# Sliding-window attention with a highway layer: keys on the partitions, values over 128 rows, a cast v that is moved on chip

## The chip, the cores and the metric

The kernel runs on one core of one Trainium2 chip. The metric is the device time of one execution in microseconds; the kernel before took 182.04 us (median of 3 runs, 181.88 to 184.85). TensorE (PE in the profile) multiplies, VectorE (DVE), ScalarE (ACT) and GpSimd (POOL) work on elements, SyncE (SP) only issues DMAs here. Each engine takes its instructions strictly in the order in which they were written for it.

## The reference

```python
B, H, S, D = 8, 8, 576, 64                 # q, k, v: float32
scores = q @ k.T / sqrt(D)
rel = pos[:, None] - pos[None, :]          # query minus key
slopes = 2.0 ** (-8.0 * (arange(H) + 1) / H)
mask = (rel >= 0) & (rel < 128)            # causal, a window of 128
attn = softmax(where(mask, scores - slopes * abs(rel), -1e9))
x = (attn @ v) as (4608, 512)              # heads side by side
H = relu(x @ w_h)                          # w_h, w_t: 512 x 512
T = sigmoid(x @ w_t + b_t)
out = T * H + (1 - T) * x                  # float32
```

A query sees its own key and the 127 before it, so a tile of 128 keys matters to 256 queries at most.

## The kernel before, in words

The work is cut into batches b (8) and, in a batch, key tiles u of 128 keys (u = 0 to 3, and u = 4 with 64 keys: 40 units) and output blocks of 128 tokens. There are 36 blocks: four whole ones a batch, and a fifth (tau = 4) for each pair of batches, which holds the last 64 tokens of both. All matrices are bf16.

Loads. `load_qk` (L115 to L123) fetches q and k on POOL's DMA queue and turns them to bf16 on the way; `load_v` (L125) fetches v as float32 on SP's queue, two neighbouring tokens in each partition; `cast_v` (L132) turns it to bf16 in the tile `va`, which has a column of ones beside each head so that the row sums of the softmax come out of the same matmul. `tr` (L216) transposes q and k on DVE, so that 32 pairs of features stand on the partitions of each head: four heads j fill 128 partitions, h says which four.

Scores, `scores` (L227). For a unit, 32 matmuls of 32 rows by 64 columns of the array (L235): t picks the even or the odd keys, e the half of the features, h the half of the heads. The 64 keys of one t stand on 64 partitions of PSUM, and h decides which 64. Then 16 matmuls of 32 by 32 (L244) add the mask and the ALiBi slope from a table. The result takes four PSUM banks (`sc`, one buffer), so the scores of a unit can't begin before the exponential of the last unit has read them. `soft` (L250) is that exponential on ACT, PSUM to bf16.

Values, `pv` (L265). A block takes the unit of its own tokens and the one before. Since the even and odd keys of four heads stand on 64 partitions, its matmuls (L287) are 64 rows deep: 32 for a block with two units, 16 for tau = 0, 64 for tau = 4. `norm` (L299) divides by the row sums on DVE, `x_tr` (L308) transposes the block by four matmuls, `x_copy` (L314) takes that to SBUF on ACT or DVE. The tile `av` (PSUM, one buffer) holds both the values and the transposed block.

The highway layer. `mm_z` (L333) and `mm_h` (L344) are four matmuls of 128x512 each. The bias enters z by a copy on ACT before them (`bias`, L319) or by a matmul (`bias_mm`, L323). Then `tanh` on ACT, `relu_sub`, `to_gate`, `gate` and `add_x` on DVE and POOL, and `store` (L367) on SP's queue.

What sets the order. The string ORDER (L14) is a list of words written out by hand, one for each step above: the letter names the step (S scores, E exponential, P values, N norm, U transpose, X or x copy on ACT or DVE, Z or z the z matmuls with the bias by ACT or by matmul, H, Y tanh, R, O, G or g, A or a, D store, T transposes of q and k, C or c cast of v, V, Q, L loads), the digits its place. Nothing reorders it. On SP's queue the loads of v and the stores stand in one line, and a store that waits for its block holds back all that is behind it.

Of the kernel before, what the change touches and what calls it, by code (L numbers as in the profile page):

```python
# [9 lines left out]
P = 128  # L10
NB, NU, NJ = 8, 5, 4
# [3 lines left out]
Q011 V000 V001 V011 V010 J L02 L10 L12 i0 Q010 i1 Q000 Q001 L00 K I T0111 T0100 T0101 T0110 V021  # L15
T0001 T0000 T0011 V020 T0010 V030 M S00 V031 F C01 E00 c00 w02 S01 w03 W11 w10 Q111 P00 E01 N00
Q100 U00 X00 S02 W00 P01 E02 W01 N01 W13 H00 V200 Q101 T1111 U01 S03 Q110 X01 R00 W12 E03 T1110
H01 V120 V110 V100 V101 T1001 C02 V111 P02 T1000 z00 N02 T1011 S04 Y00 U02 R01 z01 X02 V121
T1010 H02 C03 V130 T1101 Y01 V040 Q21 E04 T1100 P03 V131 Q20 O01 S10 V221 N03 V141 E10 C10 V041
g01 U03 z02 x03 A01 O00 R02 V140 Y02 G00 P10 S11 N10 B03 A00 H03 E11 O02 g02 U10 A02 T2101 Z03  # L20
T2110 X10 S12 C11 R03 V201 Y03 C12 P11 E12 O03 z10 N11 G03 T2100 U11 A03 H10 X11 V211 T2000 D00
Y10 P12 V210 R10 B11 S13 D02 N12 V220 V400 H11 C14 V300 E13 O10 D01 C13 T2111 U12 Z11 V311 G10
T2011 X12 D03 S14 Y11 R11 V310 P13 Q31 E14 T2001 z12 V301 A10 N13 V240 H12 V230 Y12 Q30 T2010
U13 C04 O12 S20 X13 O11 R12 G11 P14 E20 z13 N14 A11 c20 U14 Y13 G12 S21 x14 T3111 P20 E21 A12
z14 N20 C22 D12 H13 V231 T3100 D10 C21 Y14 O13 U20 R13 S22 X20 T3110 B20 G13 P21 E22 D11 Z20 N21
A13 H14 O14 T3011 Q40 D13 V340 V320 U21 V321 S23 R14 X21 V401 Y20 T3010 P22 G14 V420 E23 z21 N22
A14 T3001 U22 S24 X22 C23 T3000 H20 Y21 C31 T3101 E24 P23 C30 O20 B22 S30 R20 Q41 N23 H21 G20
E30 O21 U23 Z22 R21 A20 g21 X23 S31 T4001 A21 Y22 P30 T4000 E31 z23 D21 V330 V421 N30 V331 V410
H22 T4011 Y23 U30 O22 C32 V411 S32 X30 R22 V440 P31 T4010 G22 E32 V241 z30 N31 V341 A22 D14 O23
U31 H23 T4110 D20 X31 C33 V431 c42 Y30 P32 Q50 R23 B31 S33 N32 G23 H30 E33 O30 U32 A23 R30 Z31  # L30
X32 T4100 S34 C24 D23 D22 V521 V430 P33 T4101 E34 G30 H31 N33 Y31 A30 z32 R31 T4111 H32 C34 Y32
O31 Q51 U33 g31 S40 X33 R32 A31 O32 P34 E40 g32 D31 V501 V540 V601 T5000 V500 z33 A32 V610 D30
N34 H33 C43 D32 Y33 C40 O33 U34 S41 R33 X34 C41 B34 T5001 G33 P40 H34 E41 N40 A33 V511 Z34 T5011
V510 V541 U40 R34 Q61 S42 V731 X40 T5010 D33 C50 Y34 P41 V710 E42 O34 z40 T5100 G34 N41 H40 A34
Y40 T5111 U41 S43 X41 R40 Q60 z41 E43 O40 T5101 G40 P42 T5110 S44 A40 N42 H41 E44 Y41 T6101 D40
U42 V520 V730 S50 X42 R41 P43 O41 E50 G41 z42 N43 V611 c51 A41 U43 D34 Y42 S51 x43 V630 O42 P50
V441 E51 z43 N50 V640 T6110 V531 U50 H42 C52 V600 Y43 T6010 V530 X50 S52 R42 V621 P51 T6100 G42
E52 V631 z50 N51 V620 D41 A42 T6111 U51 H43 X51 O43 Q70 Y50 P52 R43 C61 B51 S53 N52 G43 Z51 E53
T6011 C53 U52 H50 T6001 A43 X52 O50 S54 Y51 R50 P53 Q71 E54 z52 N53 C44 C54 V741 V641 V700 D42
g50 V701 H51 Y52 T6000 A50 U53 O51 S60 X53 R51 C73 B53 P54 g51 E60 O52 A51 H52 N54 Z53 C60 D51  # L40
V711 R52 V740 D43 V721 U54 T7000 G52 S61 X54 T7010 Y53 P60 A52 T7001 H53 E61 N60 C62 z54 D52 D50
C63 O53 R53 U60 S62 X60 g53 Y54 T7110 A53 P61 E62 z60 N61 C70 T7101 U61 C74 H54 Y60 O54 X61 S63
R54 P62 T7011 E63 G54 z61 N62 A54 T7111 S64 H60 E64 T7100 D54 D53 V720 Y61 U62 O60 S70 R60 X62
B62 g60 P63 O61 A60 E70 H61 N63 Z62 C64 R61 U63 g61 Y62 H62 a61 X63 O62 S71 B63 R62 P70 E71 g62
H63 N70 A62 Z63 R63 C71 D62 D61 D60 U70 Y63 S72 C72 x70 O63 P71 E72 g63 z70 N71 A63 U71 H70 D63
X71 Y70 P72 R70 B71 S73 N72 H71 E73 O70 g70 U72 Z71 A70 x72 R71 P73 Y71 D70 S74 N73 z72 E74 O71
g71 U73 Y72 H72 x73 A71 O72 P74 R72 D71 z73 N74 G72 U74 Y73 A72 H73 x74 z74 R73 D72 O73 H74 g73
Y74 A73 O74 R74 D73 g74 a74 D74
# [4 lines left out]
def kernel(  # L53
# [27 lines left out]
    NEG = 1.0e6  # L81
# [19 lines left out]
    VA = [cp.tile([P, NU, NJ, 2, D + 1], BF16, name=f"va{i}") for i in range(4)]  # L101

    PR = [cp.tile([P, NJ, 2, 256], BF16, name=f"pr{i}") for i in range(5)]
    PS = [cp.tile([P, NJ, 2, 256], BF16, name=f"ps{i}") for i in range(2)]
# [5 lines left out]
    ident = cp.tile([P, P], BF16, name="ident")  # L110

    SI = cp.tile([P, 2, 32], BF16, name="si")
    MT = cp.tile([P, 2, 320], BF16, name="mt")
# [18 lines left out]
    def cast_v(b, u, eng):  # L132
        eng.tensor_copy(  # L133
            out=VA[b % 4][:, u, :, :, 0:D],
            in_=VS[b % 3][:, u].rearrange("p j (t d) -> p j t d", t=2))
# [16 lines left out]
    def split_b():  # L152

        nc.vector.memset(one[:], 1.0)
        nc.vector.memset(bR[:], 0.0)
# [278 lines left out]
```

## Time and profile before

| | |
|---|---|
| time, median of 3 runs | 182.04 us |
| the profiled execution's own time | 180.61 us |
| its span, first to last instruction | 178.7 us |
| mean granted clock of TensorE | 0.981 |
| busy: PE, DVE, ACT, POOL | 141.2, 131.7, 103.7, 100.8 us |
| matmuls that the trace holds | 3490 |
| moved by DMA | 31.17 MB, 224 GB/s of HBM traffic |

The time of a run is about 1.9 us more than the span of its profile, which covers the instructions alone. Busy time is summed over the whole span, so it mixes the start (loads), a long steady part and the end (the last blocks). Matmuls are pipelined: a busy PE may still be waiting for weights, and a row's duration is longer than the distance from one row's start to the next. That distance is what the engine spends.

### The profile page before, as it was taken

Reading aid. Unit: us, or ns where it says so; the run is one execution under the profiler, and the core shown is the slowest. Engines: PE = TensorE matmul, PEld = TensorE weight load, DVE = VectorE, ACT = ScalarE, POOL = GpSimd, SP = SyncE. Lnnn points to the kernel's source line nnn. Section 1 sums busy time; section 2 is a strip of 40 time slices with the busy share of each in tenths; the row PEclk is TensorE's granted clock in tenths of the full one; section 3 lists DMA queues with packets and bytes.
Section 4 is the critical chain, followed back from the end, with each engine's and each line's share of the span. In section 5 each row is a group of like instructions: output and inputs, shape, how many; then the busy total and the mean of one; then the engine's idle time right before and its main releaser. Section 6 shows DMA issues by size and latency. Waiting matters only on the chain.

```text
span 178.7 us, 7880 instructions
## 1 busy us (share of the span) xinstructions
PE 141.2 (79%) x3490; PEld 80.8 (45%) x3529; DVE 131.7 (74%) x276; ACT 103.7 (58%) x117; POOL 100.8 (56%) x125
## 2 busy tenths in 40 slices
PE   0004559988999897699998998999779999999940
PEld 0002335544556454355555555545455555555510
DVE  4757938977886877277989986578669778857680
ACT  2000557566877687188755885778375858775210
POOL 6203590067797679536858986349576653522720
PEclk9999999999999999699999999999999999999996
DMA  4999999993789759905998999948986305151132
GB/s 79 215 259 369 217 171 223 227 188 106 226 188 183 201 168 205 189 31 178 166 299 147 286 187 257 280 138 207 162 212 199 121 4 150 55 187 62 59 117 61
DMA packets 30641, 31.17 MB, mean 174 GB/s; under 512 B 2320, under 2 KB 20752, under 8 KB 30608
## 3 DMA queue, kind: packets, MB, share of 16 engines
q1 hardware_dynamic: 26192, 21.24, 40.1%
q0 software_dynamic: 4416, 9.44, 32.1%
q8 instruction: 27, 0.44, 1.0%
q14 instruction: 6, 0.05, 0.1%
HBM read 30.67 MB, written 9.44 MB: 224 GB/s over the span
## 4 chain that ended last, share of the span: by engine, by line
PE 75%; issue 8%; DMA 6%; DVE 5%; POOL 2%; ACT 1%; POOLq 0%
PE h L348 18%; PE z L336 17%; PE av L287 13%; PE sc L235 12%; PE sc L244 7%; DMA ld<-in_q_dram 6%; PE av L311 5%; PE z L325 3%; ACT pr L258 1%; POOL ld L121 1%; DVE wH L147 1%; DVE vs L205 1%; DVE va L133 0%; DVE wT L147 0%; DVE tr L218 0%
## 5 line engine op out<-in xcount | busy, mean ns | idle before, releaser
L258 ACT ACTIVATE pr<-sc 128x2048 bf16<-128x2048 f32 (+2 forms) x32 | 53.3, 1664 | 37.6 <-PE sc L244 37.6
L365 POOL TENSOR_TENSOR ot<-uu,x 128x512 f32<-128x512 bf16 x34 | 39.4, 1158 | 26.6 <-DVE uu L361 16.4
L218 DVE STREAM_TRANSPOSE tr<-ld 128x288 uint32<-128x288 uint32 x64 | 41.9, 707 | 4.0 <-DMA ld<-in_k_dram 2.6
L235 PE MATMUL sc<-tr,tr 32*64 32x256 bf16 (+2 forms) x1280 | 27.5, 280 | 19.1 <-DVE tr L218 15.9
L348 PE MATMUL h<-wH,xt 128*128 128x512 bf16 x128 | 36.9, 386 | 1.2 <-issue 0.6
L336 PE MATMUL z<-wT,xt 128*128 128x512 bf16 x128 | 34.0, 379 | 2.1 <-issue 1.2
L361 POOL TENSOR_TENSOR uu<-uu,tt 128x512 bf16<-128x512 bf16 x20 | 23.1, 1156 | 17.0 <-DVE uu L353 12.3
L133 POOL CAST va<-vs 128x512 bf16<-128x512 f32 x36 | 21.8, 627 | 17.6 <-DMA vs<-in_v_dram 17.6
L353 DVE SCALAR_TENSOR_TENSOR uu<-h,x 128x512 bf16<-128x512 f32 x36 | 24.7, 687 | 9.0 <-PE h L348 8.4
L342 ACT ACTIVATE tt<-z 128x512 f16<-128x512 f32 x36 | 21.5, 598 | 15.2 <-PE z L336 15.0
L235 PEld LDWEIGHTS <-tr 32*64 32x64 bf16 x1280 | 17.8, 140 | 27.1 <-issue 12.7
L287 PE MATMUL av<-va,pr 64*128 64x65 bf16 (+1 forms) x960 | 23.1, 195 | 5.9 <-issue 5.4
L304 DVE TENSOR_TENSOR x<-av,rd 128x512 bf16<-128x512 f32 x36 | 24.9, 692 | 1.3
L287 PEld LDWEIGHTS <-pr 64*128 64x128 bf16 (+1 forms) x960 | 18.3, 98 | 14.2 <-issue 9.0
L316 ACT COPY xt<-av 128x512 bf16<-128x512 bf16 x29 | 17.0, 585 | 10.8 <-PE av L311 9.9
L303 DVE RECIPROCAL rd<-av 128x8 f32<-128x8 f32 x36 | 7.3, 202 | 20.7 <-PE av L287 20.5
L336 PEld LDWEIGHTS <-xt 128*128 128x128 bf16 x144 | 13.7, 98 | 13.6 <-issue 0.9
L357 DVE TENSOR_SCALAR tt<-tt 128x512 f16<-128x512 f16 x36 | 17.8, 497 | 2.3 <-ACT tt L342 2.2
L348 PEld LDWEIGHTS <-xt 128*128 128x128 bf16 x144 | 12.6, 99 | 13.5 <-issue 2.3
L244 PE MATMUL sc<-mt,si 32*32 32x512 bf16 (+2 forms) x640 | 16.5, 364 | 0.0
L311 PE MATMUL av<-ident,x 128*128 128x128 bf16 x144 | 14.3, 222 | 2.4 <-DVE x L304 1.9
L311 PEld LDWEIGHTS <-x 128*128 128x128 bf16 x144 | 10.1, 99 | 11.9 <-DVE x L304 5.7
(46 smaller groups left out, 82.6 us busy)
## 6 DMA issues: line engine op xcount, KB each, us to landing
vs<-in_v_dram SPq DMA_DIRECT2D x64, 128.0 KB, 5.1
out_dram<-ot SPq DMA_DIRECT2D x32, 256.0 KB, 3.3
ld<-in_k_dram POOLq DMA_DIRECT2D x6, 576.0 KB, 7.5
ld<-in_q_dram POOLq DMA_DIRECT2D x6, 576.0 KB, 8.1
ld<-in_k_dram POOLq DMA_DIRECT2D x4, 288.0 KB, 6.2
ld<-in_q_dram POOLq DMA_DIRECT2D x4, 288.0 KB, 8.0
vs<-in_moe_w_h_dram SPq DMA_DIRECT2D x2, 512.0 KB, 12.6
vs<-in_moe_w_t_dram SPq DMA_DIRECT2D x2, 512.0 KB, 12.1
```

Source lines behind the costliest of these rows:

```text
L218: nc.vector.transpose(out=t[:, 0:S, :].rearrange("p s e -> p (s e)").bitcast(U32).rearrange("p (s t) -> p t s", t=NT)[:, 9 * part : 9 * pa ...
L235: nc.tensor.matmul(out=sc[64 * h : 64 * h + 64, j, 256 * t : 256 * t + n], lhsT=TR[b % 2, 1, h][rows, k0 : k0 + 127 : 2, e], rhs=TR[b % 2, ...
L244: nc.tensor.matmul(out=sc[32 * c : 32 * c + 32, j, :].rearrange("p (t n) -> p t n", t=2)[:, :, 0:n], lhsT=SI[rows, c // 2, :], rhs=MT[rows ...
L258: nc.scalar.activation(out=p[:, :, :, 0:n], in_=SC.pop((b, u))[:].rearrange("p j (t n) -> p j t n", t=2)[:, :, :, 0:n], func=ACTF.Exp, sca ...
L287: nc.tensor.matmul(out=av[o : o + m, h, 65 * j : 65 * j + 65], lhsT=PT[bb, u][rows, j, 1 - t, off : off + m], rhs=VA[bb % 4][rows, u, j, t ...
L304: nc.vector.tensor_tensor(out=x[:].rearrange("p (h j d) -> p h j d", h=2, j=NJ), in0=av[:, :, :, 0:D], in1=rd[:].to_broadcast([P, 2, NJ, D ...
L311: nc.tensor.transpose(out=AV[blk][:, c // 2, 272 + 64 * (c % 2) :][:, 0:64].bitcast(BF16), in_=X[blk][:, c * P : (c + 1) * P], identity=id ...
L336: nc.tensor.matmul(out=pz[:], lhsT=xt[:, c * P : (c + 1) * P], rhs=wT[:, c, :], start=False, stop=c == NC - 1, skip_group_check=True)
L348: nc.tensor.matmul(out=pa[:], lhsT=xt[:, c * P : (c + 1) * P], rhs=wH[:, c, :], start=c == 0, stop=c == NC - 1)
L353: nc.vector.scalar_tensor_tensor(out=uu[:], in0=PA.pop(blk)[:], scalar=0.0, in1=X[blk][:], op0=ALU.max, op1=ALU.subtract)
L361: eng.tensor_tensor(out=UU[blk][:], in0=UU[blk][:], in1=TT.pop(blk)[:], op=ALU.mult)
L365: eng.tensor_tensor(out=ot[:], in0=UU.pop(blk)[:], in1=X.pop(blk)[:], op=ALU.add)
```

## The change

It does five things.

**Keys on the partitions.** A unit's 128 keys now stand on the 128 partitions of PSUM in their own order. A score matmul is 32 rows by 128 columns of the array (L248), so there are 16 of N = 256 for a unit where there were 32. The mask and bias table is built for this order (`mt`), and its slope is in the table instead of in the weights.

**Units 3 and 4 in one.** The last 64 keys of a batch share the PSUM tile of unit 3: 16 matmuls of N = 192, 16 of N = 64, one set of 16 bias matmuls (from a table of its own, `mx`), one exponential. There are 32 units instead of 40, all with 2048 columns.

**Values over 128 rows.** `pv` (L306) uses all 128 partitions: 16 matmuls for a block with two units, 8 for tau = 0, 32 for tau = 4, the last ones 64 columns wide, in two column halves that alternate.

**A cast v that is moved.** v still comes with two neighbouring tokens in each partition, but keys now stand one in each partition. So `cast_v` writes a tile `vg`, and `move_v` (44 DMAs on SP's queue) carries it to `va`, 64 rows a DMA: token parity t goes to every second partition. 12 of the 40 casts are on ACT, 28 on POOL (before: 4 on DVE, 36 on POOL).

**Another order of issue.** Most q and k transposes are one instruction instead of two (28 whole, 8 halves; before 64 halves). 14 x copies are on DVE instead of 7, 20 bias copies on ACT instead of 11 (so 16 bias matmuls instead of 25). There are four buffers `pr` and one `ps`, before five and two. The clearing of buffers moves from DVE to POOL.

On PE, what stands about the last units of batch 0, before (h is the highway matmul, av the values or the transposes, si the bias weights, mt the bias table; rows that alternate are left out):

```order
L311 MATMUL av<-ident,x 128x128
L235 LDWEIGHTS tr_87
L235 MATMUL sc<-tr_85,tr_87 64x192
...
L244 MATMUL sc<-mt,si 32x2x192
L348 LDWEIGHTS xt
...
L235 MATMUL sc<-tr_85,tr_87 64x64
...
L244 MATMUL sc<-mt,si 32x2x64
L311 LDWEIGHTS x
```

and of the change:

```order
L306 MATMUL av<-va_98,pr_102 128x65
L248 LDWEIGHTS tr_87
L248 MATMUL sc<-tr_85,tr_87 128x192
...
L248 MATMUL sc<-tr_86,tr_88 128x64
L258 LDWEIGHTS eye
L258 MATMUL sc<-mx,eye 32x512
L324 LDWEIGHTS x
```

Two visits to the scores, each with its own bias matmuls, have become one.

On SP's queue, from the first store of a pair's shared block on (batches 0 and 1), before (vs is v as loaded, ot a finished block):

```order
L376 DMA out_0_dram<-ot_1659 64x512 x2
L372 DMA out_0_dram<-ot_1840 128x512
L127 DMA vs1_94<-in_v_dram 64x4x128
L372 DMA out_0_dram<-ot_2176 128x512
L372 DMA out_0_dram<-ot_2050 128x512
```

and of the change, there and a little later:

```order
L389 DMA out_0_dram<-ot_1400 64x512 x2
L385 DMA out_0_dram<-ot_1342 128x512
L143 DMA va0_98<-vg0_96 64x1300 x2
L132 DMA vs2_95<-in_v_dram 64x4x128
L385 DMA out_0_dram<-ot_1435 128x512
L132 DMA vs2_95<-in_v_dram 64x4x128
L143 DMA va0_98<-vg0_96 64x1300
```

The four moves of a batch stand in the same line as the stores and the loads. From batch 2 on each carries the whole batch's 5 units for one parity and one half of the heads.

On POOL, the start, before:

```order
L121 DMA ld01_80<-in_k_dram 128x1152
L174 ISA
L174 IOTA pi_115 32x1 x4
L176 IOTA qi_116 128x321
L177 AFFINE_SELECT ident_112<-ident_112 128x128
L121 DMA ld01_80<-in_k_dram 128x1152
L121 DMA ld00_79<-in_q_dram 128x1152 x2
```

and of the change:

```order
L217 MEMSET vs_94 128x512
L217 MEMSET vs_93 128x512
L126 DMA ld_79<-in_q_dram 128x1152 x2
L226 MEMSET vg_96 128x40
L226 MEMSET vg_97 128x40
L180 ISA
L180 IOTA pi 32x1 x4
L182 IOTA qi 128x352
L183 AFFINE_SELECT ident<-ident 128x128
L126 DMA ld_80<-in_k_dram 128x1152 x2
```

Two clears now stand ahead of the first load of q, and the loads of k behind the index tables.

The diff, cut to its core (the ORDER string is replaced as a whole; its first line is shown):

```diff
-Q011 V000 V001 V011 V010 J L02 L10 L12 i0 Q010 i1 Q000 Q001 L00 K I T0111 T0100 T0101 T0110 V021
+i2 L02 M1 V001 M0 V000 Q001 J V011 Q000 V041 I V040 i0 V031 V021 Q011 i1 L10 Q010 W02 F c00 f
...
-    VA = [cp.tile([P, NU, NJ, 2, D + 1], BF16, name=f"va{i}") for i in range(4)]
+    VG = [cp.tile([P, 2, NU, NJ, D + 1], BF16, name=f"vg{i}") for i in range(2)]
+    VA = [cp.tile([P, 2, NU, NJ, D + 1], BF16, name=f"va{i}") for i in range(4)]
...
     def cast_v(b, u, eng):
-        eng.tensor_copy(
-            out=VA[b % 4][:, u, :, :, 0:D],
-            in_=VS[b % 3][:, u].rearrange("p j (t d) -> p j t d", t=2))
+        (eng.copy if eng is nc.scalar else eng.tensor_copy)(
+            out=VG[b % 2][:, :, u, :, 0:D],
+            in_=VS[b % 3][:, u].rearrange("p j (t d) -> p t j d", t=2))
+
+    def move_v(b, u0, u1, t, half):
+        nc.sync.dma_start(
+            out=VA[b % 4][t::2, half, u0:u1].rearrange("r u j d -> r (u j d)"),
+            in_=VG[b % 2][64 * half : 64 * half + 64, t, u0:u1].rearrange("r u j d -> r (u j d)"))
...
     def scores(b, u):
         sc = SC[b, u] = ps_sc.tile([P, NJ, 512], F32, name="sc")
-        n = min(256, S - P * u)
-        for t in range(2):
+        parts = [(u, 0, 256)] if u < 3 else [(3, 0, 192), (4, 192, 64)]
+        for kt, col, n in parts:
             for e in range(2):
                 for h in range(2):
                     for j in range(NJ):
...
-                            out=sc[64 * h : 64 * h + 64, j, 256 * t : 256 * t + n],
-                            lhsT=TR[b % 2, 1, h][rows, k0 : k0 + 127 : 2, e],
-                            rhs=TR[b % 2, 0, h][rows, P * u : P * u + n, e],
...
-                            tile_position=(32 * j, 64 * h))
+                            out=sc[:, j, 256 * h + col : 256 * h + col + n],
+                            lhsT=TR[b % 2, 1, h][rows, P * kt : P * kt + P, e],
+                            rhs=TR[b % 2, 0, h][rows, P * kt : P * kt + n, e],
...
+                            skip_group_check=True, tile_position=(32 * j, 0))
...
-                    lhsT=SI[rows, c // 2, :], rhs=MT[rows, :, off : off + n], start=False,
...
+                    lhsT=eye[rows, :],
+                    rhs=MT[rows, :, off : off + 256] if u < 3 else MX[rows, c],
...
     def pv(blk):
...
-                lhsT=PT[bb, u][rows, j, 1 - t, off : off + m],
-                rhs=VA[bb % 4][rows, u, j, t, :], start=first, stop=True,
-                skip_group_check=True, tile_position=(64 * h, o))
...
+                out=av[o : o + m, h, 65 * j : 65 * j + 65], lhsT=PT[bb, pt][:, j, h, off : off + m],
+                rhs=VA[bb % 4][:, h, u, j, :], start=(h, o) not in seen, stop=True,
+                skip_group_check=True, **kw)
```

More of the change, by code (lines that the diff above doesn't have):

```diff
@@ L10 @@
 P = 128
[L11 removed]
+NB, NU, NJ, NPR = 8, 5, 4, 4
 ORDER = """
[L15 to L19 removed]
@@ L207, in k_clear, with v_clear @@
+    def v_clear(b):
+        nc.gpsimd.memset(VS[b][:, 4], 0.0)
     def k_clear():
@@ L263, with warm @@
+    def warm(n):
+        pz = ps_f.tile([P, DM], F32, name="z")
+        for _ in range(n):
+            nc.tensor.matmul(out=pz[:], lhsT=one[:], rhs=nil[:], start=True, stop=True)
     PZ, XT, PA, TT, UU, OT = {}, {}, {}, {}, {}, {}
     def pv(blk):
-        calls = []
-        b, tau = blk
-        if True:
-            av = AV[blk] = ps_av.tile([P, 2, 512], F32, name="av")
-            terms = [(b, tau, 0, 0, P)]
-            if tau:
-                terms.append((b, tau - 1, P, 0, P))
-            if tau == 4:
-                terms = [(bb, u, off, 64 * i, 64) for i, bb in enumerate((b - 1, b))
-                         for u, off in ((4, 0), (3, P))]
-            seen = set()
-            for bb, u, off, o, m in terms:
-                for j in range(NJ):
-                    for t in range(2):
-                        for h in range(2):
-                            calls.append((bb, u, off, o, m, j, t, h, (h, o) not in seen))
-                            seen.add((h, o))
@@ L285, in one_mm @@
[L285 to L297 removed]
+        b, tau = blk
```

225 lines of the change are left out of this document (120 added, 105 removed).

## The prediction

> **What bounds the kernel now.** First the page: its parts on busy time and on the chain that ended last.
>
> ```profile
> span 178.7 us, 7880 instructions
> PE 141.2 (79%) x3490; PEld 80.8 (45%) x3529; DVE 131.7 (74%) x276; ACT 103.7 (58%) x117; POOL 100.8 (56%) x125
> PE 75%; issue 8%; DMA 6%; DVE 5%; POOL 2%; ACT 1%; POOLq 0%
> ```
>
> DVE's share is almost PE's, but the chain is PE for 75% and "issue" for 8% more, so the shares don't say who waits. The view of waits on PE does:
>
> ```profile
> PE sc L235 <- DVE tr L218: 15.9, 2, 14.0
> PE av L287 <- issue: 5.4, 4, 2.4
> PE sc L235 <- ACT pr L258: 2.0, 1, 2.0
> PE av L311 <- DVE x L304: 1.9, 1, 1.9
> PE z L336 <- issue: 1.2, 7, 0.2
> PE sc L235 <- issue: 1.2, 2, 0.6
> PE h L348 <- issue: 0.6, 3, 0.2
> PE av L287 <- ACT pr L258: 0.5, 1, 0.5
> ```
>
> The timeline puts the first, third and fourth of these into the start, and shows where the start and PE's work end:
>
> ```profile
> 14.04 0.43 PE L235 MATMUL sc<-tr,tr 32*64 32x256 bf16 x4 [14.04 <-DVE tr L218]
> 16.31 1.07 PE L235 MATMUL sc<-tr,tr 32*64 32x256 bf16 x28 [1.84 <-DVE tr L218]
> ...
> 20.00 1.08 PE L235 MATMUL sc<-tr,tr 32*64 32x256 bf16 x32 [2.04 <-ACT pr L258]
> ...
> 24.12 0.61 PE L311 MATMUL av<-ident,x 128*128 128x128 bf16 x4 [1.90 <-DVE x L304]
> ...
> 170.85 1.03 PE L348 MATMUL h<-wH,xt 128*128 128x512 bf16 x4
> ```
>
> Between 24.1 and 171.9 us PE waits for another engine once, 0.5 us. What is left is its own work and "issue". So a microsecond less on PE there is a microsecond less in the end, as long as the others keep up. What that work costs is read from starts, not from durations:
>
> ```profile
> 81.05 0.39 PE L311 MATMUL av<-ident,x 128*128 128x128 bf16 x4
> 81.37 0.69 PE L235 MATMUL sc<-tr,tr 32*64 32x256 bf16 x32
> 81.99 0.43 PE L244 MATMUL sc<-mt,si 32*32 32x512 bf16 x16
> 82.35 0.69 PE L287 MATMUL av<-va,pr 64*128 64x65 bf16 x32
> ...
> 84.08 0.40 PE L311 MATMUL av<-ident,x 128*128 128x128 bf16 x4
> 84.31 1.03 PE L348 MATMUL h<-wH,xt 128*128 128x512 bf16 x4
> 85.27 0.69 PE L287 MATMUL av<-va,pr 64*128 64x65 bf16 x32
> 85.89 0.58 PE L235 MATMUL sc<-tr,tr 32*64 32x192 bf16 x32
> 86.40 0.38 PE L244 MATMUL sc<-mt,si 32*32 32x384 bf16 x16
> 86.72 1.04 PE L348 MATMUL h<-wH,xt 128*128 128x512 bf16 x3
> 87.59 0.39 PE L311 MATMUL av<-ident,x 128*128 128x128 bf16 x4
> ...
> 88.77 0.45 PE L235 MATMUL sc<-tr,tr 32*64 32x64 bf16 x32
> 89.15 0.27 PE L244 MATMUL sc<-mt,si 32*32 32x128 bf16 x16
> 89.35 0.69 PE L287 MATMUL av<-va,pr 64*128 64x65 bf16 x32
> ```
>
> From start to start: scores of a whole unit 0.62, its bias matmuls 0.36; unit 3 0.51 and 0.32; unit 4 0.38 and 0.20; values 0.62; four highway matmuls 0.87 (one of the four is missing at 86.72), 0.22 each. The four transposes cost 0.23 before dense matmuls (84.08) but 0.32 before scores (81.05): going from one shape of array tile to another costs 0.09. The highway matmuls show it too, 0.96 before values. So of the 0.62 of the values (85.27) 0.09 is the way out, and their 16 pairs go every 0.033.
>
> **The change part by part.** The sum is made against the profiled execution, 180.61 us; the median of the runs is 182.04, 1.4 more, and I add that at the end.
>
> Whole units: nothing. Before, a unit's 32 score matmuls are four passes of eight, each pass 256 columns on eight tiles at once. Now they are four passes of four, still 256 columns, on tiles twice as wide. Half the instructions, the same columns streamed: 0.62 stays, if the wider weights load behind the stream as the narrow ones do. I also leave the values' 16 deep matmuls at the 0.033 of the 16 pairs.
>
> (A) Units 3 and 4 in one. Before 0.51 + 0.32 + 0.38 + 0.20 and one change of shape, 0.09: 1.50. Now 0.36 for one full set of bias matmuls, and scores between 0.62 (the row with the same columns in all) and 0.89 (0.51 + 0.38). I take 0.75, the middle, since the extra passes are real but fill and drain come once. That is 1.11: 0.39 less, 8 times, 3.1 us (2.0 to 4.2).
>
> (B) Values at full height have the shape of the dense matmuls about them. Counted in ORDER, 11 ways into values from dense matmuls and 27 out of them were changes of shape; 5 stay, about the four shared blocks. 33 x 0.095 = 3.1 us.
>
> (C) The shared blocks: 64 matmuls become 32, 16 pairs fewer at 0.033, four times: 2.1 us.
>
> (D) Nine bias matmuls fewer at 0.22: 2.0 us.
>
> (E) Issue. The longest stall and what follows it:
>
> ```profile
> 70.52 0.22 PE L287 MATMUL av<-va,pr 64*128 64x65 bf16 x3
> 73.12 0.56 PE L287 MATMUL av<-va,pr 64*128 64x65 bf16 x13 [2.38 <-issue]
> 73.61 1.08 PE L235 MATMUL sc<-tr,tr 32*64 32x256 bf16 x32
> 74.63 0.65 PE L244 MATMUL sc<-mt,si 32*32 32x512 bf16 x16
> ...
> q8 instruction: 27, 0.44, 1.0%
> ```
>
> PE stops in the middle of one run of matmuls, waiting for nothing, and then runs slow: scores 1.02 instead of 0.62. The instruction queue moves 0.44 MB in 27 packets, 16 KB each, and PE's program has 7060 rows, 62 bytes a row: a packet is some 260 rows. I read the stalls as PE out of instructions. The waits are 8.4 us in the rows above; the seven of 0.2 at z stand where bias matmuls are missing from the trace, which leaves 7, and the slow stretches after them add about 1. Now there are 4354 rows, 17 packets. In proportion 3 of the 8 us go. But the dense runs thin out as well: scores, bias and values were 160 rows in 1.6 us and are 96 in 1.5, so a packet lasts 4.1 us there instead of 2.6. If that ends all stalls, 8 go. I take 6.
>
> The Trainium skill, in Runtime: NRT & Kernel Launch, Instruction fetch mechanics, agrees on blocks of 16 KiB, and says of the sequential prefetch that "ifetch is hidden" by the issue rate. By that rule (E) is nothing; the 2.38 us above speak against it.
>
> (F) The start. POOL now clears two 128x512 tiles ahead of the first load of q, and the loads of k come behind its tables. The nearest rows for the price, with those for the next parts:
>
> ```profile
> L133 POOL CAST va<-vs 128x512 bf16<-128x512 f32 x36 | 21.8, 627 | 17.6 <-DMA vs<-in_v_dram 17.6
> L321 ACT COPY z<-bB 128x512 f32<-128x512 f32 x11 | 6.6, 596 | 0.2
> ...
> vs<-in_v_dram SPq DMA_DIRECT2D x64, 128.0 KB, 5.1
> out_dram<-ot SPq DMA_DIRECT2D x32, 256.0 KB, 3.3
> ...
> SPq L372 <- POOL ot L365: 53.4, 15, 10.8
> ```
>
> Two at a cast's 0.63 are 1.3 us for the first load; the later ones queue behind it anyway, and DVE gives up clears of its own. 0 to 1.3; I take 0.7 lost.
>
> (G) The moved v. Its lead is this: by the PE costs above, 2.8 to 5 us of matmuls stand between a batch's last move and its first values (2.8 for batch 6), and the cast is some 5 to 7 us ahead. The moves have no row of their own. They land between a store's 3.3 and a load's 5.1 after issue. Late by 0 to 2.3 us, at 8 places: 0 to 18 us. The nearer row is the store, which also reads rows of 2 KB from SBUF, and most moves can start before their place in ORDER, since SP runs ahead. 0.5 each: 4 us lost. Behind a late first value stand its block's whole chain and, PE being in order, all later scores.
>
> (H) The others. ACT gains nine bias copies (5.4 us), 12 casts at about 0.63 (7.5) and a few table copies, and loses seven x copies (4.2, at a bias copy's 0.6): some 114 us busy. DVE loses clears and four casts and gains seven short copies: about the same 130. Over 170 us that is 67% and 76%, where PE waited for neither before. PE's own work hides it; where it shows, it shows as short waits before the transposes and the values. 1 us lost (0 to 6).
>
> The same chain as before carries start and tail (PE's end to the last store, 6.8 us). Sum: 3.1 + 3.1 + 2.1 + 2.0 + 6 - 0.7 - 4 - 1 = 10.6 us less: 170.0, and with 1.4 for the median 171.4 us.
>
> **The rivals.** *Weight loads bound the values.* Dense 128x128 matmuls with weights of their own are in the trace once, the transposes, 57 ns apart (84.08). That may be their 128 columns or their weights. If it is the weights, 448 deep matmuls cost 24 ns more each: 10.8 us, 182 us. For it: no row shows a 128-row load faster. Against: in the pairs every half of the array gets new weights of 128 columns every 33 ns. The Trainium skill goes further in TensorE: Matmul & The Clock Gate, LDWEIGHTS: columns / 1.2 GHz, which is 107 ns; an estimate by that alone is 33 us more. The trace already undercuts it at 33 ns, which the page's section on fast weight load allows for. Chance 0.08.
>
> *Slower: the moves stand behind stores that wait.* SP's stores waited 53.4 us for POOL in 15 waits, 3.6 each, and the moves are now in that line. If at each of the 8 places one such wait comes on top, that is 29 us, less the 4 counted: 196 us. It turns the change into a loss from 1.8 us a place ((10.6 + 4) / 8). Against: the move's place in ORDER is past the store's block by then. Chance 0.07.
>
> *The stalls stay.* If "issue" is not a shortage of instructions, (E) falls away: 177.4 us. Chance 0.12.
>
> *Another engine becomes the bound.* PE's stretch of 148 us shrinks by 16, ACT's and DVE's work doesn't; if their chains through the single buffers sc and av (scores, exponential, scores; values, norm, transpose, copy, values) are now the slower ones in a part of the blocks, the 6 us of (H) are due: 176.4 us. For it: ACT's casts now stand in line with the exponentials. Chance 0.13. That leaves 0.60 for the forecast.
>
> **How the numbers follow.** The forecast alone goes from 163 (A at 4.2, E at 8, no losses: 19.4 less) to about 177. With the stalls, another engine and part of the late moves or slow weights it goes to 181; beyond lie 0.05 to 0.1 on the upper side and as much below 163. Within 2% (what a measurement of this kernel tells from no change) is 178.4 to 185.7. Faster than that: the forecast, most of the stalls and of the other engine, 0.81. Same: the weight loads, the ends of the others, 0.12. Slower: 0.07.
>
> **What would show it.** Right: whole-unit scores still 0.62 from start to start, unit 3's 0.75; values 0.53 with no 0.09 about them; q8 at 17 packets, issue waits on PE under 3 us; first scores at 16 to 17 us; PE's last matmul to the end still 7. Wrong: values at 0.9 (weights); waits of PE av for a DMA of va over 10 us in all, or SP waits that put a move behind a store (moves); issue as long as before; waits of PE for ACT or DVE above 5 us after the start.

## The result, and the profile after

The change is slower: 190.99 us (median of 4 runs, 189.78 to 197.74) against 181.96 for the kernel before on the same chip, a ratio of 1.0478 with a 95% interval of 1.0372 to 1.0583. Ratios leave disturbed runs out; where there were too few undisturbed ones for a ratio, median and range are given. The forecast was 171.4 (163 to 181).

The page of the changed kernel, its parts on busy time, on the chain that ended last and on the DMA queues:

```profile
span 188.3 us, 5259 instructions
PE 139.6 (74%) x2176; PEld 73.9 (39%) x2176; DVE 125.5 (67%) x233; ACT 112.7 (60%) x132; POOL 100.9 (54%) x127
DMA 48%; PE 26%; SPq 8%; POOL 7%; DVE 6%; issue 3%; POOLq 0%; DVEq 0%
q1 hardware_dynamic: 29712, 26.57, 50.7%
q8 instruction: 17, 0.28, 0.6%
```

Before, the chain was PE for 75% and DMA for 6%. Now it is DMA for 48%. The instruction queue has the 17 packets that were forecast. The waits on PE:

```profile
PE av L306 <- DMA va<-vg: 19.1, 12, 4.5
PE sc L248 <- DVE tr L231: 16.9, 1, 16.9
PE av L324 <- DVE x L317: 3.7, 6, 1.1
PE sc L248 <- ACT pr L271: 2.0, 1, 2.0
```

No wait for "issue" is left, where there were over 8 us. In its place the values wait 12 times for a moved v, 19.1 us in all, the row that the prediction named as a sign that the moves had gone wrong. Who held the moves up is in the waits of SP's queue and of the casts:

```profile
SPq L143 <- POOL vg L138: 21.8, 6, 8.7
SPq L143 <- ACT vg L138: 21.3, 7, 5.9
SPq L385 <- POOL ot L378: 13.2, 6, 5.4
...
POOL vg L138 <- DMA vs<-in_v_dram: 22.8, 8, 5.7
ACT vg L138 <- DMA va<-vg: 4.8, 1, 4.8
ACT vg L138 <- DMA vs<-in_v_dram: 4.6, 3, 2.2
```

SP stood 43 us with a move whose cast wasn't done (the first two rows), and the casts in turn waited for v, 27 us in the rows of POOL and ACT, where the kernel before had 17.6 (ACT's other row, 4.8 us, is a cast that waited for a move to land). The waits of stores for their blocks fell from 53.4 to 13.2: SP now spends that time at the moves. One such stop, in the timelines of SP's queue and of PE:

```profile
74.30 0.72 SPq L132 DMA_DIRECT2D vs<-in_v_dram  x1
80.31 2.44 SPq L143 DMA_DIRECT2D va<-vg  x4
82.79 1.33 SPq L132 DMA_DIRECT2D vs<-in_v_dram  x2
```

```profile
84.39 0.38 PE L306 MATMUL av<-va,pr 128*128 128x65 bf16 x4 [4.55 <-DMA va<-vg]
85.06 0.40 PE L306 MATMUL av<-va,pr 128*128 128x65 bf16 x4 [0.29 <-DMA va<-vg]
85.27 1.90 PE L349 MATMUL z<-wT,xt 128*128 128x512 bf16 x4
86.96 1.91 PE L361 MATMUL h<-wH,xt 128*128 128x512 bf16 x4
88.66 0.57 PE L324 MATMUL av<-ident,x 128*128 128x128 bf16 x4
89.17 0.64 PE L248 MATMUL sc<-tr,tr 32*128 32x256 bf16 x16
89.74 0.43 PE L258 MATMUL sc<-mt,eye 32*32 32x512 bf16 x16
90.10 0.69 PE L306 MATMUL av<-va,pr 128*128 128x65 bf16 x16
90.63 0.38 PE L338 MATMUL z<-bR,one 128*128 128x512 bf16 x1
```

SP issues nothing from 75.0 to 80.3, then four moves, 0.61 each, and only then the next loads of v, for the batches after. PE stands for 4.55 us. After that its matmuls of 512 columns take 0.43 from start to start (85.27 to 86.96 for four) where they take 0.215 otherwise.

### The profile page after: what moved, and what is told of

It is laid out like the page before. It is cut to its first block, busy times and chain, and to the rows that moved or that the text cites. A ratio compares the mean times of both kernels' runs of the same rounds, so it can differ in the third digit from the quotient of the medians.

```text
span 188.3 us, 5259 instructions
## 1 busy us (share of the span) xinstructions
PE 139.6 (74%) x2176; PEld 73.9 (39%) x2176; DVE 125.5 (67%) x233; ACT 112.7 (60%) x132; POOL 100.9 (54%) x127
## 4 chain that ended last, share of the span: by engine, by line
DMA 48%; PE 26%; SPq 8%; POOL 7%; DVE 6%; issue 3%; POOLq 0%; DVEq 0%
DMA va<-vg 14%; DMA vs<-in_v_dram 14%; DMA ld<-in_k_dram 9%; PE z L349 6%; DMA vs<-in_moe_w_t_dram 6%; PE h L361 6%; DMA out_dram<-ot 5%; PE av L306 4%; SPq L132 4%; PE sc L248 4%; SPq L143 3%; POOL vg L138 3%; PE av L324 2%; PE sc L258 2%; POOL ot L378 1%
## 5 line engine op out<-in xcount | busy, mean ns | idle before, releaser
L271 ACT ACTIVATE pr<-sc 128x2048 bf16<-128x2048 f32 x28 | 52.6, 1877 | 8.5 <-PE sc L258 8.5
L231 DVE STREAM_TRANSPOSE tr<-ld 128x576 uint32<-128x576 uint32 (+1 forms) x36 | 39.2, 1128 | 10.0 <-DMA ld<-in_k_dram 6.6
L349 PE MATMUL z<-wT,xt 128*128 128x512 bf16 x144 | 40.8, 410 | 0.0
L306 PE MATMUL av<-va,pr 128*128 128x65 bf16 (+1 forms) x480 | 23.6, 198 | 19.8 <-DMA va<-vg 19.1
L248 PE MATMUL sc<-tr,tr 32*128 32x256 bf16 (+2 forms) x640 | 22.0, 264 | 18.9 <-DVE tr L231 16.9
L374 POOL TENSOR_TENSOR uu<-uu,tt 128x512 bf16<-128x512 bf16 x21 | 24.3, 1155 | 18.4 <-DVE tt L370 14.9
L138 POOL CAST vg<-vs 128x512 bf16<-128x512 f32 x28 | 17.1, 634 | 25.6 <-DMA vs<-in_v_dram 22.8
L306 PEld LDWEIGHTS <-pr 128*128 128x128 bf16 (+1 forms) x480 | 19.1, 102 | 28.6 <-issue 12.6
L248 PEld LDWEIGHTS <-tr 32*128 32x128 bf16 x640 | 12.8, 96 | 24.3 <-DVE tr L231 16.9
L329 ACT COPY xt<-av 128x512 bf16<-128x512 bf16 x22 | 12.9, 586 | 14.6 <-PE av L324 14.0
L370 DVE TENSOR_SCALAR tt<-tt 128x512 f16<-128x512 f16 x36 | 17.6, 493 | 3.0 <-ACT tt L355 2.8
L324 PEld LDWEIGHTS <-x 128*128 128x128 bf16 x144 | 10.4, 102 | 15.4 <-DVE x L317 9.3
L138 ACT CAST vg<-vs 128x512 bf16<-128x512 f32 x12 | 7.1, 620 | 9.5 <-DMA va<-vg 4.8
## 6 DMA issues: line engine op xcount, KB each, us to landing
va<-vg SPq DMA_DIRECT2D x24, 162.5 KB, 3.3
```

What stands on the lines that cost most here:

```text
L138: (eng.copy if eng is nc.scalar else eng.tensor_copy)(out=VG[b % 2][:, :, u, :, 0:D], in_=VS[b % 3][:, u].rearrange("p j (t d) -> p t j d" ...
L231: nc.vector.transpose(out=t[:, 0:S, :].rearrange("p s e -> p (s e)").bitcast(U32).rearrange("p (s t) -> p t s", t=NT)[:, t0:t1, :], in_=ld ...
L248: nc.tensor.matmul(out=sc[:, j, 256 * h + col : 256 * h + col + n], lhsT=TR[b % 2, 1, h][rows, P * kt : P * kt + P, e], rhs=TR[b % 2, 0, h ...
L271: nc.scalar.activation(out=p[:].rearrange("p j h n -> p j (h n)"), in_=SC.pop((b, u))[:], func=ACTF.Exp, scale=scale)
L306: nc.tensor.matmul(out=av[o : o + m, h, 65 * j : 65 * j + 65], lhsT=PT[bb, pt][:, j, h, off : off + m], rhs=VA[bb % 4][:, h, u, j, :], sta ...
L324: nc.tensor.transpose(out=AV[blk][:, c // 2, 272 + 64 * (c % 2) :][:, 0:64].bitcast(BF16), in_=X[blk][:, c * P : (c + 1) * P], identity=id ...
```

## The experiments

The theories at first: **A**, a moved v is late because of its own way; **B**, a move that waits for its cast holds up the loads of v and the stores behind it in SP's line; **C**, ACT, DVE or the new order are the bound. After the first four runs (without moves, moves unread, loads of v ahead, v loaded one key a partition) **D** came in: 44 more DMAs cost something by themselves, by SP's time or by traffic.

### No moves

```diff
-            out=VG[b % 2][:, :, u, :, 0:D],
+            out=VA[b % 4][:, :, u, :, 0:D],
...
     def move_v(b, u0, u1, t, half):
+        return
```

> The cast writes straight into va and there are no moves, so keys and values no longer match; all else, the order of issue too, is the change's. Theory A (the moved v itself comes too late: transit on the DMA queue) and theory B (the moves hold up SP's line, so the next batch's loads of v, its casts and then its moves come late) both say: the 19 us of waits for va go, and with them some 8 us of half clock after them: 163 to 169 us. Rival C (ACT, DVE or the new order bound the kernel and the waits for va only hide that): 178 us or more, with waits of PE for ACT or DVE in their place.

168.13 us (164.61 to 173.12). The page's first row, and the longest waits on PE:

```profile
span 166.5 us, 5171 instructions
```

```profile
PE sc L245 <- DVE tr L228: 16.5, 1, 16.5
PE av L321 <- DVE x L314: 4.7, 6, 1.7
PE h L358 <- DVE uu L363: 4.2, 2, 4.0
PE sc L245 <- ACT pr L268: 2.0, 1, 2.0
```

Everything but the moves gives, by the median, what the prediction's sum gives without its term (G), 170.0 - 4 + 1.4 = 167.4. C falls as the cause of the loss. The moves cost 191.0 - 168.1 = 23 us by the medians, 25 between the fastest runs (189.8 and 164.6).

### The moves, but nobody reads them

```diff
-                rhs=VA[bb % 4][:, h, u, j, :], start=(h, o) not in seen, stop=True,
+                rhs=VG[bb % 4][:, h, u, j, :], start=(h, o) not in seen, stop=True,
```

(with four tiles `vg`)

> All 44 moves are issued as in the change, but the values are taken from the cast tile vg (four buffers instead of two), so nobody waits for a move and keys and values don't match. Theory A: close to the kernel without moves, at most 3 us more. Theory B: SP still stands at each move until its cast is done and the loads of v behind it are late, so the casts are late and PE waits for casts: at least 176 us, with long waits of POOL's casts for v.

191.81 us (187.95 to 194.97). No value waits for a move here, and nothing is gained by the median, 1.8 us by the fastest run: A alone falls. The waits go elsewhere. The casts wait 41 us for v, an ACT that stands 9 us with a cast delays a tanh, and PE waits for it:

```profile
PE av L324 <- DVE x L317: 11.0, 8, 5.9
PE z L338 <- ACT tt L355: 8.3, 1, 8.3
...
ACT vg L138 <- DMA vs<-in_v_dram: 21.5, 4, 9.0
POOL vg L138 <- DMA vs<-in_v_dram: 19.6, 7, 6.0
```

### The loads of v ahead of the moves, and v loaded one key a partition

From batch 3 on, the words V of batch b stand right behind the moves of batch b - 2 in ORDER:

```diff
-k12510 Y03 V241 P11 E12 V221
+k12510 V330 V300 V331 V341 V310 V301 V321 V311 V340 V320 Y03 V241 P11 E12 V221
...
-k20511 V330 O11 U13
+k20511 V441 V440 V401 V410 V420 V400 V411 V431 V421 V430 O11 U13
```

> The change as it is, but on SP's queue the loads of v for batch b (3 to 7) stand right behind the moves of batch b-2 instead of behind those of b-1. Theory A: as slow as the change, 187 to 193 us, since every move still has its short lead. Theory B: casts no longer wait for v (22.8 us of such waits now go under 5) and the time falls to 170 to 178 us.

197.96 us (196.32 to 201.73), a ratio of 1.0869 (1.0746 to 1.0992): against B's forecast. Two things go wrong. Batch 3's loads go ahead of those that batch 2 still needs, whose casts wait 12 us. From then on casts hardly wait for v, but SP still waits 47 us with a move for a cast, because POOL is late: its additions wait 19.6 us for a free tile, whose store stands behind the moves.

The other run takes moves and order away:

```diff
-            in_=v[b, 4 * half : 4 * half + 4, 128 * u : 128 * u + 2 * n].rearrange(
-                "j (p t) d -> p j (t d)", t=2))
+            in_=v[b, 4 * half : 4 * half + 4, 128 * u : 128 * u + n].rearrange("j p d -> p j d"))
```

> v is loaded with one token in each partition (256-byte runs where there were 512-byte ones), the cast writes va, there is no move. Theories A and B: 164 to 170 us if the loads keep up; each load is 512 runs instead of 256, so its 5.8 us may grow to 8, which costs a few us where a cast waits for it. Rival C: 178 us or more.

173.0 us (170.3 to 175.68), a ratio of 0.9443 (0.9316 to 0.957). v comes in runs of 256 bytes instead of 512, the casts write `va`, and there are no moves. It beats both kernels. An issue of a v load takes SP 0.89 us on the mean, where it takes 0.71 in the kernel without moves.

### Are the waits the price, or the DMAs themselves?

Moves of a constant tile to one that nobody reads, at the same places: they wait for no cast.

```diff
-            out=VA[b % 4][t::2, half, u0:u1].rearrange("r u j d -> r (u j d)"),
-            in_=VG[b % 2][64 * half : 64 * half + 64, t, u0:u1].rearrange("r u j d -> r (u j d)"))
+            out=VB[b % 2][t::2, half, u0:u1].rearrange("r u j d -> r (u j d)"),
+            in_=VG[0][64 * half : 64 * half + 64, t, u0:u1].rearrange("r u j d -> r (u j d)"))
```

> Casts write the tile that the values read, as in the kernel without moves (168.1 us), so keys and values don't match. The 44 moves are issued at their places with their sizes, but from a tile that is written once at the start to tiles that nobody reads: they wait for no cast. Theory B (the moves cost what they hold up in SP's line while they wait for casts): 168 to 172 us, SP's line waits for stores only, no wait of POOL or ACT for v above 10 us in all. Theory D (44 issues of some 0.6 us on SP and 5.3 MB more of traffic are the price, whatever they wait for): 180 us or more, with casts that wait for v as with the change (27 us).

181.77 us (178.94 to 184.02), ratio 0.9799 (0.9666 to 0.9933). This is D's number, with no wait for a cast in SP's line; the casts wait 29.6 us for DMAs, where 14.9 do without moves. More than half of the 23 us comes without B. To tell SP's time from traffic, the same with 16 bytes a row:

```diff
-            out=VB[b % 2][t::2, half, u0:u1].rearrange("r u j d -> r (u j d)"),
-            in_=VG[0][64 * half : 64 * half + 64, t, u0:u1].rearrange("r u j d -> r (u j d)"))
+            out=VB[b % 2][t::2, half, u0, 0, 0:8],
+            in_=VG[0][64 * half : 64 * half + 64, t, u0, 0, 0:8])
```

> As the kernel with constant moves (181.8 us; without moves 168.1), but each of the 44 moves carries 16 bytes a row (64 rows) instead of up to 2600, so SP still issues 44 more DMAs and the traffic is gone. Keys and values don't match, as there. If SP's issue time is the price: 177 us or more, and casts wait for v 20 us or more in all. If the traffic of 5.3 MB on the DMA engines is the price: 167 to 171 us, with the DMA queue's share back near the 46% of the kernel without moves.

180.56 us (178.34 to 182.94), ratio 0.9974 (0.9911 to 1.0036): the bytes of the moves cost nothing that these runs can tell, their number costs it all. The other side of that test halves the stores' bytes in the change:

```diff
-            nc.sync.dma_start(out=out[row : row + P, :], in_=ot[:])
+            nc.sync.dma_start(out=out[row : row + P, 0:256], in_=ot[:, 0:256])
```

> The change, but each store writes only the first 256 of 512 columns of its block, so half of the output is left out: 4.7 MB less traffic, about what the moves add (5.3), with the same number of issues, waits and words. If traffic on the DMA engines is most of the loss: 176 to 182 us. If the waits in SP's line (a move for its cast, loads and stores behind it) or the place of the moves in the order are most of it: 187 to 191 us, with PE's waits for va still above 15 us.

192.7 us, ratio 1.0538 (1.0394 to 1.0682), PE's waits for va 20.8 us. Again not the bytes. How many DMAs does it take, then? The tiny moves of one parity only, 22:

```diff
     def move_v(b, u0, u1, t, half):
+        if t:
+            return
```

> The kernel with 44 moves of 16 bytes a row (180.6 us; without moves 168.1), with 22 of them: those of one token parity only. Keys and values don't match, as there. If each DMA in SP's line has its price: half of the 12.5 us, 172 to 177 us. If the line has room for some and breaks down beyond a number: 170 us or less, or 178 and more, with the casts' waits for v near those of the kernel without moves (12 us) or near those of the 44 (35 us).

170.75 us (167.84 to 172.6), ratio 0.9278 (0.9172 to 0.9384). Neither forecast fits fully, but the price isn't a price for each: by the medians 22 DMAs cost some 2.6 us (3.2 between the fastest runs, within the spread of the kernel without moves) and the next 22 about 10. The waits of the casts, first with 22, then with 44:

```profile
POOL va L139 <- DMA vs<-in_v_dram: 13.1, 7, 5.6
ACT va L139 <- DMA vs<-in_v_dram: 2.3, 1, 2.3
```

```profile
ACT va L139 <- DMA vs<-in_v_dram: 17.7, 5, 6.3
POOL va L139 <- DMA vs<-in_v_dram: 17.1, 5, 8.9
...
SPq L387 <- POOL ot L380: 24.4, 9, 6.4
SPq L133 <- DMA vs<-in_v_dram: 12.8, 7, 3.1
SPq L144 <- DMA vs<-in_v_dram: 8.6, 5, 2.7
```

15.4 us with 22, hardly more than the 14.9 without any (all waits of casts that a DMA ended); 34.8 with 44, as with the real moves (34). So v is late once SP's line is too full. The last two rows are SP waiting for older DMAs. Where the late v hurts is one stop above all, which is in the kernel with 44 and not in that with 22. PE's wait, SP's line before it, and ACT's casts:

```profile
PE z L340 <- ACT tt L357: 6.8, 1, 6.8
```

```profile
46.12 6.14 SPq L133 DMA_DIRECT2D vs<-in_v_dram  x7
```

```profile
56.80 0.62 ACT L139 CAST va<-vs 128x512 bf16<-128x512 f32 x1 [4.75 <-DMA vs<-in_v_dram]
60.25 0.62 ACT L139 CAST va<-vs 128x512 bf16<-128x512 f32 x1 [2.83 <-DMA vs<-in_v_dram]
```

A tanh stands behind these casts, and PE waits for it. Of the seven loads of v, the last four were issued from 49.2 to 51.3 us, beside POOL's loads of q and k (576 KB each, from 49.0 and 49.8), and took 7.5 to 10.0 us to land. Without moves the seven were issued from 41.3 to 45.1, ahead of such a pair (47.3 and 48.1), and had all landed by 49.6. So 44 DMAs brought these loads into a stretch where loads took 10 us. That POOL's loads are why is likely, but no run moves them away.

Why SP waits for older DMAs, the built program says: each of SP's DMAs waits for one of eight semaphores in turn, that is until the eighth DMA before it has landed (order of the changed kernel, with waits):

```
97 L143 DMA va_98<-vg_96 64x1300 [waits DMAHW1_49,PE_49,Pool_49]
98 L143 DMA va_98<-vg_96 64x1300 [waits DMAHW2_49,PE_49]
99 L132 DMA vs_95<-in_v_dram 64x4x128 [waits DMAHW3_49]
100 L385 DMA out_dram<-ot 128x512 [waits DMAHW4_49]
```

The trace shows the same eight in turn. Counted from issues and landings, no DMA on SP's queue starts with more than seven others under way, and with just seven start 20 of 125 in the kernel before, 31 of 125 without moves, 53 of 169 with the tiny ones.

Had the kernel before room in that line? 44 DMAs of 16 bytes a row put into it, 10 for each of the first two batches and 4 for each of the others:

```diff
+    def tiny(b, u):
...
+        nc.sync.dma_start(out=VB[i % 2 : P : 2, i, 0:8], in_=VC[64 * (i // 2 % 2) : 64 * (i // 2 % 2) + 64, i, 0:8])
```

> The kernel before with 44 tiny DMAs of 16 bytes a row on SP's queue, from one constant tile to one that nobody reads, at places like those of the moves (batch 0 after its first values). If SP's line was full only because the change made PE faster: 181 to 185 us. If the line was at its limit in the kernel before too: 189 us or more, with casts that wait for v.

190.53 us (185.65 to 194.56): slower by 8.4 us by the medians (190.5 and 182.1) and 5.0 between the fastest runs (185.7 and 180.7). The median meets the second forecast and the fastest run lies between the two, so there was little room in this line before the change. The run that its profile holds is the fastest of the four. There the casts wait 28.0 us for v where they waited 17.6, and PE waits for casts, which it didn't before:

```profile
POOL va L148 <- DMA vs<-in_v_dram: 28.0, 8, 11.3
PE av L303 <- POOL va L148: 5.2, 3, 4.1
```

### Another engine for a part of the line

Five runs take something out of SP's line. The moves to POOL, in the change:

```diff
     def move_v(b, u0, u1, t, half):
-        nc.sync.dma_start(
+        nc.gpsimd.dma_start(
```

> The change, but the 44 moves are issued by POOL at the same places of the order, so that SP's line holds loads and stores only. POOL issues for about 0.76 us a DMA (its loads of q), 33 us more for an engine with 101 us busy; 28 of the 40 casts are its own, so its line waits only for ACT's 12. Theory B: 171 to 180 us, casts no longer wait for v (under 8 us in all), PE's waits for a moved v under 8 us where the change had 19. Theory D, for the traffic: 186 to 192 us. If the moves' own way (issue to landing, 3.3 us) is enough by itself: PE still waits 15 us or more for va though casts are on time.

191.69 us, ratio 1.0465 (1.0369 to 1.0562). POOL's casts wait 7.8 us for v, so SP's line is free, and the stores wait 67.5 us in it as of old. But PE waits as long for va as with the change, the last outcome that the expectation names. So SP's line is not the only way to lose these microseconds: here a moved v is late though its cast is on time:

```profile
PE av L306 <- DMA va<-vg: 18.1, 7, 5.2
...
POOL vg L138 <- DMA vs<-in_v_dram: 7.8, 4, 3.4
```

The loads of v to ACT, from batch 2 on:

```diff
     def load_v(b, u, half):
...
-        nc.sync.dma_start(
+        (nc.sync if b < 2 else nc.scalar).dma_start(
```

> The change, but from batch 2 on the loads of v are issued by ACT at the same places of the order; SP's line holds stores and moves. ACT pays some 0.6 us for each of 60 loads, 36 us more for an engine with 113 us busy. Theory B in its narrow form (the loop goes through the loads: a move waits for a cast, the next loads wait behind it, the next casts for them): casts wait for v under 8 us in all and the time falls to 174 to 182 us. If the loop goes through the stores (a store behind a waiting move, no free tile for a block, POOL stalled, its casts late): 186 to 194 us, with POOL waiting for stores above 10 us. Theory D (SP's issue time): falls as well, since SP issues 60 DMAs fewer; D's traffic: stays at 186 or above with no long wait on SP.

200.73 us (196.69 to 201.53). The stores to POOL, `nc.sync` to `nc.gpsimd` in both lines of `store`:

> The change, but the stores are issued by POOL at the same places of the order, right behind or soon after POOL's own additions; SP's line holds loads and moves. POOL pays about 0.76 us for each of 40 stores, 30 us more. If the loop goes through the stores: 172 to 182 us, and POOL no longer waits for stores. Theory B in its narrow form (through the loads): 186 to 193 us, with casts waiting for v 20 us or more in all, since loads still stand behind moves. Theory D for SP's issue time: falls by several us; for the traffic: no change.

196.66 us (188.04 to 202.06). Neither gains. In the first, the built program shows that ACT's DMAs take their turns in the same eight semaphores as SP's, so that ACT waits for SP's line and its exponentials with it. In the second the casts wait only 14 us for v, but SP still waits 54 us with moves for casts. The tiny moves issued by POOL (`nc.gpsimd` in `move_v`), and by ACT (`nc.scalar`):

> The 44 moves of 16 bytes a row (180.6 us when SP issues them), issued by POOL, so that neither SP's time nor its eight places for DMAs on their way are taken. Theory that these are the price: 167 to 172 us, v no longer late for the casts (under 15 us in all, as without moves). Theory that 44 more DMAs cost this wherever they are issued: 177 us or more.

> The same 44 tiny moves, issued by ACT. In the built program ACT's DMAs take their turn in the same eight semaphores as SP's, a DMA waiting for the eighth before it, but SP's issue time of some 0.65 us each is spared. Theory of the eight places: 178 us or more, and ACT waits for DMAs. Theory of SP's issue time alone: 168 to 173 us.

POOL 180.91 us, ratio 0.9957 (0.9872 to 1.0042); ACT 191.74 (188.48 to 193.66). The first is against the theory that SP's time or its eight places are the price: SP's line is free (its stores wait 59.4 us), and the time is that of SP's issue all the same. POOL has 124 us of work there instead of 101, and PE waits 10.3 us for x, 3.9 for the highway's PSUM tile and 3.2 for a bias; the casts are hardly later than without moves (16.4 us for DMAs, 14.9). That POOL is as tight a line as SP would explain it, but no run shows it apart from the other theory, that 44 more DMAs cost this wherever they are issued. In the second the forecast of the eight places came, but ACT stood so long (24.6 us in its three longest waits of exponentials and x copies for DMAs) that it doesn't separate SP's time from the eight places. That stays open.

### Earlier places

Loads, casts and moves 30 words earlier in ORDER from batch 4 on, first on SP's queue (moves of batch 3, 15 words earlier; C40 leads the casts of batch 4):

```diff
-X22 k30511 k30510 B22 O21 G20 P23 k30501 O14 E30 H21 V400 g14 A20 N23 V501 Z22 D13 R21 V411 Q41
+k30500 X21 V400 Q40 Y20 V501 P22 k30511 T3102 k30510 E23 V411 z21 N22 k30501 H20 V431 Y21 O20 U22
+V421 S30 R20 X22 V540 B22 O21 V430 G20 P23 O14 E30 H21 g14 A20 N23 Z22 C40 D13 R21
```

> The change, but from batch 4 on the loads of v, the casts and the moves all stand 30 words earlier in the order (batch 3: 15), which is some 6 us more ahead of the values that need them; their order among themselves is the same, and they go past stores, q and k loads and POOL's work. If the place is the cause (the last move stands 20 to 28 words, 3 to 5 us, ahead of the first values, and cast, issue and way take longer): PE's waits for va fall from 19 to under 9 us and the time to 180 to 184 us, about that of the constant moves, which nobody waits for. If the DMA engines simply can't carry the bytes in time, or the line's own waits move along: 188 us or more.

194.04 us, ratio 1.0586 (1.0436 to 1.0736). No gain: the casts now wait for v 36.6 us (in the slowest of its four runs, the one that the profile holds). Asking earlier didn't help in this line. Then the same with the moves on POOL:

> The change with both edits that did nothing alone: the moves issued by POOL (191.7 us), and from batch 4 on loads of v, casts and moves 30 words earlier (194.0 us). Theory of two conditions (the line of SP is too full, so that earlier places don't come earlier; with the line relieved, the places are too late for cast, issue and way): 172 to 180 us, PE's waits for va under 8 us. Theory that a move on the way from cast to values costs this much wherever it stands: 187 us or more.

184.71 us, ratio 1.0154 (1.0053 to 1.0255). Each edit alone gains nothing, both together 6 to 7 us: so the places were too late as well, once the moves were off SP's line. The 172 to 180 weren't reached. The longest waits on PE after the start:

```profile
PE av L309 <- DMA va<-vg: 12.2, 5, 4.4
...
PE av L327 <- DVE x L320: 6.3, 5, 3.3
```

PE waits 12.2 us where under 8 was expected. On POOL's queue the moves stand behind loads of q and k of 576 KB, and four moves issued at 110 to 115 us landed at 119 to 124.

### v as bf16 straight from memory

One step on from the direct load, on POOL's queue, which turns v to bf16 on the way:

```diff
+        nc.gpsimd.dma_start(
+            out=VA[b % 4][0:n, u, :, 0:D],
+            in_=v[b, :, 128 * u : 128 * u + n].rearrange("g p d -> p g d"))
```

> The direct load (173.0 us) taken one step on: POOL's DMA queue turns v to bf16 on the way, as it does q and k, one token a partition, straight into va: 40 loads, no casts, no moves. ACT loses 12 casts and POOL 28, POOL gains 40 issues of some 0.76 us or more. If reading v in runs of 256 bytes on this queue costs no more than on SP's: 164 to 172 us. If POOL's issue of so many short pieces is slow (over 2 us a load) or the queue of q and k backs up: 176 us or more, with PE waiting for va or DVE for q and k.

181.3 us, ratio 0.9984 (0.9907 to 1.0062). In this kernel some loads of batch b + 4 stand ahead of the last values of batch b, so shared blocks use another batch's v; the amount of work is the same. The second forecast came: the queue of q, k and v is busy for 76.9% of 16 engines' span, the first scores start at 24.5 us instead of 16.5, and PE waits 11.8 us for x.

## Why the prediction was wrong, point by point

**What bounds the kernel; whole units, (A) to (E).** Right, and somewhat too small. Scores of a whole unit go from 0.62 to 0.57 (0.62 was forecast), unit 3 with the new part of unit 4 takes 0.57 + 0.37 (0.75 + 0.36), values 0.52 with no change of shape about them (0.53), a shared block's 0.64 instead of 1.06 (C: 2.1 forecast, 1.7). All stalls of (E) are gone: 8 us, where 6 was taken. The kernel without moves shows the sum: 168.1 for 167.4.

**(F), the start.** First scores at 16.87, as forecast.

**(H), ACT and DVE.** Some 6 us too small: without moves PE waits 4.7 us for x and 4.2 for the highway's tile, 7 more than before (1.9, for x), where 1 was taken. The surplus of (A), (E) and the whole units covers most of it, so that the sum's closeness is in part luck.

**(G), the moved v.** This is the step that failed: "0.5 each: 4 us lost", at 8 places. It was 23 us, 2.9 a place, past the break-even of 1.8 that the slower rival named. Two things were wrong in it. It priced a move's own way ("They land between a store's 3.3 and a load's 5.1 after issue"; the 24 whole-batch moves took 3.3, but all 44 took 4.5 by the median and up to 7.3) and counted the 44 issues at nothing, "since SP runs ahead". The runs show the issues as 12 of the 23 us, of whatever size and waiting for no cast: the line had little room, in the kernel before too. SP's 53.4 us of waiting stores, read as slack, were not free time, for all that came behind them waited as well, eight DMAs at most under way. And it took the casts as given, "some 5 to 7 us ahead". With real moves SP stands for casts and the casts stand for v, and this costs 10 us more (191.8 against 181.8, both unread), while reading what is moved costs nothing on top by the medians (191.0), 1.8 us by the fastest runs. The places were too late besides: with the moves on POOL's queue, and casts on time, PE waits 18.1 us for va.

**The slower rival** came nearest in time, 196 for 191, with the right line but the direction turned round: "the moves stand behind stores that wait". They stood for casts, and loads and stores stood behind them. The other rivals: no slow weights (values 0.52), no stalls, and another engine as the bound only in the sense of (H).

The chain, then: without the moves the kernel is some 14 us faster; 44 more DMAs filled SP's line, so v came late to the casts (12 us); moves that wait for those casts stop the line that carries the next v (10 us). The 12 and the 10 are differences between kernels; the change itself doesn't have the long stop behind a tanh, and its loss shows as waits for va. PE shows 19.1 us of waits for va, and after its long stops 26 matmuls of 512 columns at 0.43 instead of 0.215, where the kernel without moves has 4 such: 22 x 0.21 = 4.6 us. Its waits for x and for the highway's tile are 5 us fewer. That makes 18.7 of the 21.8 us between the two spans (188.3 and 166.5).

Open: whether the line's limit is SP's time, some 0.6 us an issue, or the eight DMAs under way, or both together; and whether 44 DMAs cost 12 us on any engine, as the run on POOL's queue leaves possible.

## What to carry over

An engine that only issues DMAs is a line with a capacity like any other: count its issues, its waits and how many may be under way before adding to it. A queue's waiting time need not be slack when later loads stand behind the wait. A DMA that waits for a computed tile is a risk in the queue that brings the data for the next one; here a slower load straight into place (173.0 us) beat load, cast and move by 18 us.

## What was not expected of the hardware

44 DMAs of 64 rows by 16 bytes cost as much as 44 of up to 162.5 KB, 180.6 and 181.8 us. After waits of 3.1 to 4.6 us, and once after two of 1.3, PE runs for 3 to 5 us at half its rate (0.43 for 512 columns, up to 88.66 in the rows above), so a long wait costs more than its length: the granted clock was 0.50 from 44.7 to 51.5, 82.2 to 89.0, 109.5 to 112.9 and 130.0 to 133.4 us. The Trainium skill, in TensorE: Matmul & The Clock Gate, What's actually happening, gives about 3.4 us for the window that decides on this. The trace agrees, with slow stretches of one or two such windows; the two waits of 1.3 us are shorter than a window, with 0.3 us of work between them. Its DMA: Bandwidth & Descriptors, Issuing engines are not separate DMA queues, calls the time to initiate a DMA "usually small relative to the DMA itself". The trace agrees for one DMA, 0.6 us of SP beside 3.3 to landing for a whole-batch move; 44 tiny ones still made the kernel 12 us longer.
